# Attention on one Trainium2 core: two heads' scores in one tile of two banks, with one exponential over both

## The chip, the cores and the metric

The kernel runs on one core of a Trainium2 chip. The metric is the device time of one execution in microseconds (us), measured from outside the program; a few executions are made and their median is taken. The core has five engines that run at the same time and wait for each other by semaphores: TensorE (PE in the profile; PEld is its loading of weights), VectorE (DVE), ScalarE (ACT), GpSimd (POOL) and SyncE (SP), which here does nothing but start transfers (DMAs). Matmuls write to PSUM, a memory of eight banks; a bank holds 512 fp32 columns of 128 rows.

## The reference

One transformer block in fp32 on 2048 tokens of width 640: layer norm, attention with 32 heads of width 20, a residual sum, layer norm again, a SwiGLU network of width 1728 and a second residual sum. The change touches the attention alone:

```
scores = jnp.einsum("bhqd,bhkd->bhqk", q, k) * (Dh ** -0.5)
p = _softmax(scores, axis=-1)
o = jnp.einsum("bhqk,bhkd->bhqd", p, v)
h = x + o.transpose(0, 2, 1, 3).reshape(B, S, D) @ wo
h2 = h + (silu(ln(h) @ w_gate) * (ln(h) @ w_up)) @ w_down
```

## The kernel before, in words

The program has three stages: projections of queries, keys and values (which also find some of the maxima of the scores), attention, and the SwiGLU network. Each engine executes its instructions in the order in which the Python code issues them.

**Units and steps.** Attention works through 32 units (line 1040): a unit u is a group of four heads (g = u // 4) with 512 queries (c = u % 4). A unit has 16 steps, one for each tile of 128 keys (`kt`, line 1045), so there are 512 steps. In a step the scores of four heads are computed, transposed, as tiles of 128 keys by 512 queries; their exponentials go to two tiles `probs` of two heads each; and the exponentials of two steps earlier are multiplied with the values into `acc` (`weigh`, lines 972 to 980, kept back by the list `todo`).

**Maxima.** The exponential needs the largest score of each query. It is subtracted inside the score matmul: two extra rows of the queries, filled in by `max_finish`, carry the negative maximum as a sum of two parts, and the keys have rows of ones there. So while unit u is being worked on, the maxima of the next units are found: `max_one` (lines 200 to 212) multiplies 128 queries of one head with 512 keys into a bank `ps_max` and VectorE reduces it. After a unit's last maximum `max_all` (214) reduces the parts and negates them, and two steps later `max_finish` (221 to 236) transposes the result on TensorE into a PSUM tile, splits it in two parts on ScalarE and VectorE (`split`, lines 84 to 86) and writes them into the query rows with four DMAs.

**Halves of the array.** Heads are stacked two to a tile: one in rows 0 to 63 and one in rows 64 to 127 (index b = 0 or 1). A score or maximum matmul thus uses one half of TensorE's rows, and the next matmul on the other half can run beside it.

**The order in a step** is written out by hand in `ORDER` (line 41), one string for even and one for odd steps. `W` is the weighing of an older step; directly behind it come a finished maximum's `max_finish`, pieces of other work (`extra`, `preparing`). `s` and `S` are scores of a head with b = 0 and b = 1: `heads` (line 1049) makes them heads 0 and 2, and 1 and 3. `m` and `M` are maxima with b = 0 and 1. When no maxima are left the order is `sSsSW`. Before: `WsSmmSsM` and `WSsMMsSm`.

**Banks.** The attention stage has four single-bank tiles `ps_one` for scores (line 624; `max_finish` takes one as well), three `ps_max`, and one `acc`. Each score matmul (line 964) goes to a `ps_one` of its own and is read by an exponential of 512 columns (line 970). Tiles rotate: the fifth score waits until the exponential of the first is done.

**Other work that meets these steps.** After a unit's last weighing ScalarE copies `acc` to `o` (line 984); `max_finish` puts a small copy on ScalarE; POOL prepares the weights of the network; in the last units the output projection (lines 663 to 754) runs in the steps, with `ps_max` as its PSUM.

Of the kernel before, what the change touches and what calls it, by code (L numbers as in the profile page):

```python
# [9 lines left out]
F32 = mybir.dt.float32  # L10
# [3 lines left out]
AF = mybir.ActivationFunctionType  # L14
# [3 lines left out]
P = 128  # L18
# [7 lines left out]
CH = 512  # L26
NC = S // CH
TPC = CH // P
NF = (F + P - 1) // P
G = 4  # L30
# [7 lines left out]
LOWEST = -3.4028234e38  # L38
GD = G * DH

ORDER = ("WsSmmSsM", "WSsMMsSm")


@with_exitstack
def tile_block(ctx: ExitStack, tc: tile.TileContext, x, wqkv, wo, wg, wu, wd, out):
    nc = tc.nc
# [24 lines left out]
    psum = ps_ctx.enter_context(tc.tile_pool(name="psum", bufs=1, space=bass.MemoryType.PSUM))  # L71
# [4 lines left out]
    def ps_one():  # L76
        return psum.tile([P, CH], F32, name="ps_one", tag="ps_one", bufs=2)
# [6 lines left out]
    def split(src, hi, lo, lo_engine=nc.vector):  # L84
        nc.scalar.activation(hi, src, AF.Copy)  # L85
        lo_engine.tensor_tensor(out=lo, in0=src, in1=hi.bitcast(F32), op=ALU.subtract)  # L86
# [133 lines left out]

    def max_finish(u):

        m = ps_one()[: G * TPC, :P]
        nc.tensor.transpose(m, ends.pop(u), ident)
        parts = stk.tile([G * TPC, 2, P], F32R, name="m2", tag="m2", bufs=1)
        split(m, parts[:, 0], parts[:, 1], nc.vector)
        for b in range(2):
            for i in range(2):
                row = b * ROW + NPART + i
                first = b * 2 * TPC  # L230
                nc.sync.dma_start(
                    queries[u][row : row + 1].bitcast(F32).rearrange(
                        "r j (t p) -> r (j t) p", t=TPC
                    ),
                    parts[first : first + 2 * TPC, i, :].bitcast(F32),
                )
# [31 lines left out]
    with tc.tile_pool(name="pa", bufs=2) as pa:  # L268
# [138 lines left out]
        def flip(c, k):  # L407
            ps = ps_one()
            for t in range(TPC):
                nc.tensor.transpose(  # L410
                    ps[:, t * P : (t + 1) * P], xs[c * TPC + t][:, k * P : (k + 1) * P], ident
                )
            z_hi, z_lo = (z[:, k, :] for z in zs[c])
            split_sbuf(ps, z_hi, z_lo, next_e()[:, 0, :CH].bitcast(F32))
# [19 lines left out]
        def query_key(c, m):  # L434

            z_hi, z_lo = zs[c]
            ps = ps_wide()[:, 0, :] if slot[0] < 6 else ps_one()
            for n, (a, w) in enumerate(((z_hi, w_hi), (z_lo, w_hi), (z_hi, w_lo))):
                for k in range(ND):
                    nc.tensor.matmul(  # L440
                        ps, w[:, k, m * P : (m + 1) * P], a[:, k, :],
                        start=(n == 0 and k == 0), stop=(n == 2 and k == ND - 1),
                    )
                    if n == 1 and k == 3 and c:
                        visit(3)
            keep(c, m, ps)
# [117 lines left out]
        for c in range(NC):  # L564
# [7 lines left out]
            for j, (kind, *which) in enumerate(work):  # L572
# [27 lines left out]
                if 0 in ends:  # L600
                    finish_at = min(finish_at, slot[0] + 2)
                    if slot[0] == finish_at:
                        max_finish(0)
# [17 lines left out]
    ps_ctx = ExitStack()  # L621
    psum = ps_ctx.enter_context(tc.tile_pool(name="psum_a", bufs=1, space=bass.MemoryType.PSUM))

    def ps_one():
        return psum.tile([P, CH], F32, name="ps_one", tag="ps_one", bufs=4)

    def ps_max():
        return psum.tile([P, CH], F32, name="ps_max", tag="ps_max", bufs=3)
# [327 lines left out]
    v_stk.append(pb.tile([P, NT, VG], F32, name="v_stk1", bufs=1))  # L956
    scale = 1.0 / math.sqrt(DH)

    def scores(u, kt, j, probs):

        p, b = divmod(j, 2)
        rows = slice(b * ROW, b * ROW + NPART + 2)
        ps = ps_one()
        nc.tensor.matmul(  # L964
            ps,
            keys[u // NC][rows, p, kt * P : (kt + 1) * P],
            queries[u][rows, p, :],
            start=True, stop=True,
        )
        nc.scalar.activation(probs[p][:, b, :], ps, AF.Exp, scale=scale)  # L970

    def weigh(u, kt, probs, acc):
        for j in range(G):
# [66 lines left out]
    for u in range(NU):  # L1040
# [4 lines left out]
        for kt in range(NT):  # L1045
            now[0] = u * NT + kt
            ready = [v for v, at in closing.items() if at == now[0]]
            probs = [pp.tile([P, 2, CH], F32, name="probs") for _ in range(2)]
            heads = [[0, 2], [1, 3]]
            order = ORDER[now[0] % 2] if singles[0] or singles[1] else "sSsSW"  # L1050
            for op in order:
                if op in "mM":
                    next_max(int(op == "M"))
                elif op in "sS":
                    scores(u, kt, heads[op == "S"].pop(0), probs)
                else:
                    if len(todo) == 2:
                        weigh_next()
                    for v in ready:
                        max_finish(v)  # L1060
                    if extra:
                        extra.pop(0)()
                    if preparing and u and kt not in (3, 4):
                        preparing.pop(0)()
                    if now[0] == (NU - NC) * NT + 8:
                        unit_ring, last_ring = weight_rings()
                        unit_ring.fill()
                        last_ring.fill()
# [41 lines left out]
    u, o, r = tail.pop()  # L1110
# [561 lines left out]
```

## Time and profile before

| what | value |
|---|---|
| time, median of 3 runs | 2104.36 us (2101.28 to 2106.47; the runs: 2106.47, 2101.28, 2104.36) |
| span of the profiled execution, first to last instruction | 2102.6 us (the profile gives no other time of that execution) |
| instructions of the core | 37159 |
| exponentials (line 970) | 2048, 614 ns each |
| score matmuls (line 964) | 2048, 450 ns each |
| maxima: matmuls (line 204), reductions (line 210) | 1472 each, 425 and 684 ns |
| weighing (line 974) | 4096 matmul records, 604 ns each |
| output copies (line 984) | 32, 628 ns each |
| TensorE clock | full (mean 0.996) |

How to read it: the page of the profile gives the busy time of each engine, the chain of work that ended last, and groups of instructions by line. In a group's row stand the line, the engine, the operation, output and inputs, shapes and count; behind the first bar the busy time in us and the mean of one in ns; behind the second the idle time of the engine just before, with what ended it ("<-"). The mean of one is longer than the distance between two, since neighbours overlap. A row of the timeline has the start in us from the start of the span, the duration, the engine, the line and the operation; equal neighbours are merged (x2), and idle time ahead of it stands in brackets. A row of the windows has for each engine (PE, PEld, DVE, ACT, POOL) the busy time in us and the number of instructions.

### The profile page before, as it was taken

The page shows a single profiled execution, that of the slowest core. Times are in us where ns is not written, and L with a number is a line of the kernel's source. Part 1 is how long each engine was busy: PE and PEld are TensorE (multiplying, and loading weights), DVE is VectorE, ACT ScalarE, POOL GpSimd, SP SyncE. Part 2 cuts the span into 40 slices and gives each one's busy share as a digit, 9 for nine tenths or more (in the row PEclk, how much of TensorE's full clock was granted, in tenths as well). Part 3 has the DMA queues.
Part 4 walks back from the last instruction along what each step waited for, and adds up shares of the span by engine and source line. Part 5 has one row for each costly group of instructions (what it writes and reads, how often), then busy time and mean ns, then how long its engine had stood idle before and what let it go on. Part 6 is the DMA issues. An engine that isn't in the chain of part 4 may idle for free.

```text
span 2102.6 us, 37159 instructions
## 1 busy us (share of the span) xinstructions
PE 2063.2 (98%) x12636; PEld 1204.5 (57%) x12636; DVE 1659.2 (79%) x3631; ACT 1444.6 (69%) x2835; POOL 691.8 (33%) x949
## 2 busy tenths in 40 slices
PE   8899999999999999999999999999999999999998
PEld 6656566443333343333333333335578888888888
DVE  7677867788888888888888988887358666666677
ACT  4556575899999999999999999996743222212221
POOL 2131210234443434353420001001145444753555
PEclk9999999999999999999999999999999999999999
DMA  8575544335263443443631213132137755884542
GB/s 256 165 230 168 175 127 132 85 115 154 88 184 101 148 138 124 148 147 122 187 124 57 52 32 94 34 94 83 35 122 274 257 176 183 300 302 157 196 153 92
DMA packets 197285, 305.38 MB, mean 145 GB/s; under 512 B 47440, under 2 KB 82256, under 8 KB 196072
## 3 DMA queue, kind: packets, MB, share of 16 engines
q1 hardware_dynamic: 186168, 280.18, 42.0%
q10 hardware_dynamic: 10928, 22.82, 3.5%
q8 instruction: 102, 1.67, 0.3%
q14 instruction: 87, 0.71, 0.1%
HBM read 203.82 MB, written 98.30 MB: 144 GB/s over the span
## 4 chain that ended last, share of the span: by engine, by line
PE 88%; DVE 4%; DMA 3%; issue 1%; ACT 1%; POOL 1%; SPq 1%; ACTq 0%; POOLq 0%; DVEq 0%
PE acc L974 24%; PE ps_one L964 16%; PE ps_a L1135 15%; PE ps_max L204 12%; PE ps_b L1229 8%; PE ps_one L516 3%; PE ps_one L440 3%; PE ps_wide L188 3%; DVE over L195 2%; PE ps_max L695 2%; PE ps_b L695 1%; PE ps_wide L440 1%; DMA k_d<-e 1%; DMA halves<-j_d 1%; DVE mx L180 1%
## 5 line engine op out<-in xcount | busy, mean ns | idle before, releaser
L970 ACT ACTIVATE probs<-ps_one 128x512 f32<-128x512 f32 x2048 | 1056.7, 614 | 62.5 <-PE ps_one L964 37.1
L210 DVE TENSOR_REDUCE mx<-ps_max 128x1 f32<-128x512 f32 x1472 | 925.9, 684 | 108.2 <-PE ps_one L964 75.6
L964 PE MATMUL ps_one<-q_stk,k_stk 62*128 62x512 f32 x2048 | 586.1, 450 | 2.5 <-DVE m L86 1.8
L974 PE MATMUL acc<-probs,v_stk 128*32 128x512 f32 x4096 | 545.2, 604 | 0.0
L964 PEld LDWEIGHTS ps_one<-q_stk,k_stk 62*128 62x128 f32 x2048 | 251.3, 184 | 431.5 <-ACT probs L970 397.2
L204 PE MATMUL ps_max<-k_stk,q_stk 60*128 60x512 f32 x1472 | 380.8, 425 | 0.0
L204 PEld LDWEIGHTS ps_max<-k_stk,q_stk 60*128 60x128 f32 x1472 | 271.6, 186 | 25.3 <-DVE mx L210 1.2
L195 DVE CUSTOM_DVE_ANT_0 over<-ps_wide,over 128x256 f32<-128x256 f32 x512 | 185.4, 420 | 86.3 <-ACT over L193 85.9
L1350 DVE TENSOR_TENSOR tmp<-ps_a,tmp 128x512 f32<-128x512 f32 x208 | 141.1, 689 | 119.7 <-PE ps_a L1135 93.9
L193 ACT ACTIVATE over<-ps_wide 128x512 f32<-128x512 f32 x256 | 139.1, 597 | 90.5 <-PE ps_wide L188 44.1
L1229 PE MATMUL ps_b<-halves,yp 128*128 128x320 f32 x1032 | 179.3, 308 | 1.9 <-POOL yp L86 1.2
L974 PEld LDWEIGHTS acc<-probs,v_stk 128*32 128x32 f32 x4096 | 80.6, 108 | 175.4 <-issue 166.8
L1229 PEld LDWEIGHTS ps_b<-halves,yp 128*128 128x128 f32 x1032 | 165.1, 188 | 18.6 <-POOL yp L86 1.5
L1009 POOL TENSOR_TENSOR o<-o,rb 128x512 f32<-128x512 f32 x31 | 39.9, 1287 | 411.5 <-DMA q_stk<-q_d 163.6
L1135 PE MATMUL ps_a<-t,units 128*128 128x512 f32 x624 | 162.6, 396 | 0.0
L1135 PE MATMUL ps_a<-z,units 128*128 128x512 f32 x516 | 133.8, 394 | 0.0
L1135 PEld LDWEIGHTS ps_a<-t,units 128*128 128x128 f32 x624 | 112.6, 188 | 18.6
L86 POOL TENSOR_TENSOR yp<-y,yp 128x256 fp32r<-128x256 f32 x96 | 60.3, 628 | 188.0 <-ACT yp L85 188.0
L1234 DVE TENSOR_TENSOR h<-ps_b,h 128x320 f32<-128x320 f32 x248 | 110.0, 481 | 6.9 <-PE ps_b L1229 5.4
L1135 PEld LDWEIGHTS ps_a<-z,units 128*128 128x128 f32 x516 | 93.1, 187 | 15.9
L85 ACT ACTIVATE yp<-tmp 128x512 fp32r<-128x512 f32 x40 | 25.3, 632 | 103.2 <-POOL tmp L1222 103.2
L1135 PE MATMUL ps_a<-z,lasts 128*128 128x512 f32 x324 | 92.5, 393 | 0.0
(193 smaller groups left out, 2216.4 us busy)
## 6 DMA issues: line engine op xcount, KB each, us to landing
units<-w_d SPq DMA_DIRECT2D x186, 256.0 KB
w_d<-stage SPq DMA_DIRECT2D x106, 256.0 KB
halves<-j_d SPq DMA_DIRECT2D x70, 320.0 KB
j_d<-stage SPq DMA_DIRECT2D x42, 320.0 KB
k_stk<-k_d SPq DMA_DIRECT2D x64, 160.0 KB
q_stk<-q_d SPq DMA_DIRECT2D x64, 160.0 KB
rb<-r_d SPq DMA_DIRECT2D x32, 256.0 KB
raw<-k_d SPq DMA_DIRECT2D x42, 160.0 KB
```

The source lines that it names most:

```text
L193: nc.scalar.activation(over, ps[:, :, CH // 2 :], AF.Relu)
L195: nc.vector.tensor_tensor_reduce(over[:, b], ps[:, b, : CH // 2], over[:, b], 1.0, LOWEST, ALU.add, ALU.max, mx[:, b, pair, t, kc : kc + 1],)
L204: nc.tensor.matmul(ps, queries[u][rows, pair, t * P : (t + 1) * P], keys[u // NC][rows, pair, kc * CH : (kc + 1) * CH], start=True, stop=True,
L210: nc.vector.tensor_reduce(mxs[u][:, b, pair, t, kc : kc + 1], ps, axis=AX.X, op=ALU.max)
L440: nc.tensor.matmul(ps, w[:, k, m * P : (m + 1) * P], a[:, k, :], start=(n == 0 and k == 0), stop=(n == 2 and k == ND - 1),)
L964: nc.tensor.matmul(ps, keys[u // NC][rows, p, kt * P : (kt + 1) * P], queries[u][rows, p, :], start=True, stop=True,)
L970: nc.scalar.activation(probs[p][:, b, :], ps, AF.Exp, scale=scale)
L974: nc.tensor.matmul(acc[32 * j : 32 * j + 32, :], values[u // NC][:, kt, j * VW : j * VW + 32], probs[j // 2][:, j % 2, :], start=(kt == 0) ...
L1135: nc.tensor.matmul(ps.rearrange("p (t n) -> p t n", t=TPC), w[k][:, i], z[k][:, :, j], start=(first and m == 0), stop=(last and m == len(n ...
L1229: nc.tensor.matmul(ps, a, b, start=(n == 0), stop=(n == len(pairs) - 1))
L1234: nc.vector.tensor_tensor(out=h, in0=ps, in1=h, op=ALU.add)
L1350: add = lambda out, ps, x: nc.vector.tensor_tensor(out=out, in0=ps, in1=x, op=ALU.add)
```

## The change

The four single-bank tiles become two tiles of two banks, `ps_two`. The two scores that follow each other in a step, heads 0 and 1 and then heads 2 and 3, share one: each head has a bank. The first of the two takes the tile, the second is followed by one exponential of 1024 columns over both, which writes a whole `probs` tile. `both` is the list in which the function remembers the open tile. The order of a step is changed so that two maxima stand between the score pairs and one behind them. In the attention stage `max_finish` takes a `ps_max` for its transpose; the call for unit 0, which is in the stage of the projections, keeps `ps_one`. Nothing else differs.

```diff
-ORDER = ("WsSmmSsM", "WSsMMsSm")
+ORDER = ("WsSmMsSm", "WSsMmSsM")
...
     def max_finish(u):
 
-        m = ps_one()[: G * TPC, :P]
+        m = (ps_max() if u else ps_one())[: G * TPC, :P]
         nc.tensor.transpose(m, ends.pop(u), ident)
...
-    def ps_one():
-        return psum.tile([P, CH], F32, name="ps_one", tag="ps_one", bufs=4)
+    def ps_two():
+        return psum.tile([P, 2, CH], F32, name="ps_two", tag="ps_two", bufs=2)
 
     def ps_max():
         return psum.tile([P, CH], F32, name="ps_max", tag="ps_max", bufs=3)
...
+    both = []
+
     def scores(u, kt, j, probs):
 
         p, b = divmod(j, 2)
         rows = slice(b * ROW, b * ROW + NPART + 2)
-        ps = ps_one()
+        if not both:
+            both.append(ps_two())
+        else:
+            both.append(None)
+        ps = both[0]
         nc.tensor.matmul(
-            ps,
+            ps[:, b, :],
             keys[u // NC][rows, p, kt * P : (kt + 1) * P],
             queries[u][rows, p, :],
             start=True, stop=True,
         )
-        nc.scalar.activation(probs[p][:, b, :], ps, AF.Exp, scale=scale)
+        if len(both) == 2:
+            nc.scalar.activation(probs[p], ps, AF.Exp, scale=scale)
+            both.clear()
```

## The prediction

> **What bounds the kernel now.** I read the page first (engines, chain of waits, groups), then a window over the attention stage, then single steps in the timeline.
>
> ```profile
> PE 2063.2 (98%) x12636; PEld 1204.5 (57%) x12636; DVE 1659.2 (79%) x3631; ACT 1444.6 (69%) x2835; POOL 691.8 (33%) x949
> ...
> PE 88%; DVE 4%; DMA 3%; issue 1%; ACT 1%; POOL 1%; SPq 1%; ACTq 0%; POOLq 0%; DVEq 0%
> ...
> L970 ACT ACTIVATE probs<-ps_one 128x512 f32<-128x512 f32 x2048 | 1056.7, 614 | 62.5 <-PE ps_one L964 37.1
> L210 DVE TENSOR_REDUCE mx<-ps_max 128x1 f32<-128x512 f32 x1472 | 925.9, 684 | 108.2 <-PE ps_one L964 75.6
> ```
> ```profile
> 391.62:1425.80 1034.18, 1032.40 (x7201) 407.29 (x7200) 919.76 (x1524) 1003.34 (x1977) 295.61 (x460) 1.00 0.37 112
> ```
>
> In the attention stage, PE, ACT and DVE are busy 100%, 97% and 89% (1032.40, 1003.34, 919.76 of 1034.18 us): three candidates, so the shares decide nothing. So long a share of busy time on three engines only says that their work overlaps; which one sets the pace has to be read from a single step. The changed code acts only here; 1472 maxima at three a step are 490 steps. One steady step, PE first, then weight loads, then one exponential that ends before the step's scores, the first that waits for them, and the last reduction of the step before:
>
> ```profile
> 1000.78 1.06 PE L974 MATMUL acc<-probs,v_stk 128*32 128x512 f32 x8
> 1001.77 0.50 PE L964 MATMUL ps_one<-q_stk,k_stk 62*128 62x512 f32 x2
> 1002.11 0.39 PE L204 MATMUL ps_max<-k_stk,q_stk 60*128 60x512 f32 x1
> 1002.11 0.39 PE L964 MATMUL ps_one<-q_stk,k_stk 62*128 62x512 f32 x1
> 1002.34 0.50 PE L204 MATMUL ps_max<-k_stk,q_stk 60*128 60x512 f32 x2
> 1002.58 0.40 PE L964 MATMUL ps_one<-q_stk,k_stk 62*128 62x512 f32 x1
> 1002.91 0.64 PE L974 MATMUL acc<-probs,v_stk 128*32 128x512 f32 x4
> ```
> ```profile
> 1002.12 0.19 PEld L204 LDWEIGHTS ps_max<-k_stk,q_stk 60*128 60x128 f32 x1
> 1002.35 0.18 PEld L964 LDWEIGHTS ps_one<-q_stk,k_stk 62*128 62x128 f32 x1
> 1002.35 0.18 PEld L204 LDWEIGHTS ps_max<-k_stk,q_stk 60*128 60x128 f32 x1
> ```
> ```profile
> 1001.15 0.60 ACT L970 ACTIVATE probs<-ps_one 128x512 f32<-128x512 f32 x1
> ...
> 1002.31 0.60 ACT L970 ACTIVATE probs<-ps_one 128x512 f32<-128x512 f32 x1
> ```
> ```profile
> 1001.62 0.68 DVE L210 TENSOR_REDUCE mx<-ps_max 128x1 f32<-128x512 f32 x1
> ```
>
> A step is 2.13 (1000.78 to 1002.91). Call 1001.77 zero. Scores and maxima on rows 0 and 64 of the array run beside each other, so the seven matmuls take four slots, at 0, 0.34, 0.57 and 0.81, then the weighing at 1.13 (0.32 after slot 4), then 0.99 to the next zero. Slot 2 comes 0.34 after slot 1, later slots 0.23 apart: a weight load issued only when it is wanted delays its matmul by 0.11. So a matmul of slot n may have its load as late as the slot's time less 0.11, here 0.46 for slot 3 and 0.70 for slot 4. The third maximum's load, at 0.58, comes 0.05 after the reduction that frees its bank (1001.62+0.68=1002.30): 0.05 is a release. It is late but harmless.
>
> Is zero itself set by ACT? A step in which ACT is behind, and one in which DVE is:
>
> ```profile
> 425.11 0.63 ACT L984 ACTIVATE o<-acc 128x512 f32<-128x512 f32 x1
> 425.59 3.58 ACT L970 ACTIVATE probs<-ps_one 128x512 f32<-128x512 f32 x7
> ...
> 425.59 0.64 ACT L970 ACTIVATE probs<-ps_one 128x512 f32<-128x512 f32 x1
> 426.06 0.65 ACT L970 ACTIVATE probs<-ps_one 128x512 f32<-128x512 f32 x1
> ```
> ```profile
> 425.91 1.06 PE L974 MATMUL acc<-probs,v_stk 128*32 128x512 f32 x8
> ...
> 426.90 0.18 PEld L964 LDWEIGHTS ps_one<-q_stk,k_stk 62*128 62x128 f32 x2 [0.84 <-ACT probs L970]
> ...
> 427.75 0.18 PEld L964 LDWEIGHTS ps_one<-q_stk,k_stk 62*128 62x128 f32 x1 [0.31 <-ACT probs L970]
> ...
> 428.18 1.06 PE L974 MATMUL acc<-probs,v_stk 128*32 128x512 f32 x8
> ```
> ```profile
> 434.53 1.06 PE L974 MATMUL acc<-probs,v_stk 128*32 128x512 f32 x8
> ...
> 436.37 0.18 PEld L204 LDWEIGHTS ps_max<-k_stk,q_stk 60*128 60x128 f32 x1
> 436.37 0.49 PE L204 MATMUL ps_max<-k_stk,q_stk 60*128 60x512 f32 x1
> 436.79 0.16 PEld L974 LDWEIGHTS acc<-probs,v_stk 128*32 128x32 f32 x8 [0.24 <-issue]
> ```
>
> The last exponential to end before zero ended 0.02 earlier in the steady step (1001.75) and 0.19 earlier in the other (426.71 against 426.90), and weighing to zero was 0.99 both times. So the "0.84 <-ACT" there is a label on time that PE spent weighing, not a wait. A real wait is 427.75: load at 0.85, 0.11 more is 0.96 against 0.81, and that step is 2.27, 0.14 longer. Likewise 436.37 waits for DVE (finishing a unit's maximum, L217, sits ahead of the reductions): step 2.26. I take PE's own slots as the bound, ACT and DVE close behind.
>
> Beside this: the Trainium skill, "Trainium Kernel Development and Optimization", section "Best Practices", says that busy time of pipelined matmuls is no measure of the bound and that busy weight loads are. By that rule PE at 39% (407.29 of 1034.18) is free and ACT binds, which is the last rival below. The fixed 0.99 speaks against it here.
>
> **The change, part by part.** *PE's order.* s and m use one half of the array, S and M the other. The old order puts s m m s on one half and S S M on the other; the new one s m s m and S M S (mirrored in each other step). The fuller half has four matmuls either way, so four slots and 2.13: **0**. A moved maximum brings its matmul and its reduction along; the reductions still run in their old sequence of three a step, on DVE alone. A unit's last maximum issues the finishing reduction, and two steps later the transpose, its split on ACT and DVE and four row loads on SP; those stay in the step in which they were. SP and POOL keep their order, and ACT issues no DMA in this stage. If the cover were incomplete and a fifth slot appeared, it would cost 0.23 a step; nothing in the two halves calls for one.
>
> *The exponential.* Its price at 1024 columns is in no row. Nearest are
>
> ```profile
> L193 ACT ACTIVATE over<-ps_wide 128x512 f32<-128x512 f32 x256 | 139.1, 597 | 90.5 <-PE ps_wide L188 44.1 <-issue 25.0 <-DVE mx L195 7.4
> ...
> L180 DVE TENSOR_REDUCE mx<-ps_wide 128x2 f32<-128x1024 f32 x32 | 38.9, 1220 | 3.2 <-PE ps_wide L176 3.2
> ...
> L85 ACT ACTIVATE z_hi<-ps_wide 128x640 fp32r<-128x640 f32 x4 | 2.6, 705 | 4.4 <-PE ps_wide L420 4.4
> ```
>
> Back to back, an exponential of 512 costs 0.49: seven end at 429.17, the first at 426.23, 2.94/6. From 512 to 640 columns, across two banks, is 108 ns, so 512 more cost 0.43 (L180's second bank added only 536 ns to L210's 684). I take 0.92 back to back, 1.03 alone. Bounds: 0.86 (columns alone, 2x0.43) and 0.98 (nothing saved, 2x0.49). I take the middle because the 640-column row shows columns and a fixed part separately. ACT's load in a step falls from 4x0.49=1.96 to 2x0.92=1.84, but this lies beside PE's 2.13: **0** directly.
>
> By the Trainium skill, "ScalarE: Activation LUTs", section "What ACT_TABLE_LOAD costs" (186 ns plus 0.833 ns a column, 93 ns overlapped), 1024 columns would cost an estimated 0.95. The trace's 0.49 for 512 is under that page's 0.52. With 0.95 the chain below would be 2.13, just no slack left.
>
> *The new wait.* There are two tiles of two banks. Call the first score pair of a step A and the second B. A's tile was last read by the A exponential of the step before, B's by the B exponential, and only the first score of a pair carries the wait. A's exponential starts 0.54 after zero (1002.31, as the first one does now) and ends at 0.54+0.60+0.43=1.57, long before the next A. B's follows at once and ends 0.92 later, at 2.49; its banks are released at 2.54, which is 0.41 in the next step. B is in slot 3, and its load may come as late as 0.46: **0**, hidden behind the maxima of slot 2, with 0.05 to spare. Without that cover every 0.01 costs 490x0.01=5 us. Behind it on PE stand B's second score, the third maximum and the weighing. As a loop over two steps: release 0.05, load 0.11, slot 3 to 4 0.24, to the weighing 0.32, to zero 0.99, to the end of B's exponential 2.49: 4.20, or 2.10 a step under 2.13. This is the thin place of the forecast: 0.03 more per long exponential uses it up. The third maximum now has until 0.70 for its bank, which comes at 0.58.
>
> *What is late now and then.* (a) Finishing reductions, 32 in all:
>
> ```profile
> L217 DVE TENSOR_REDUCE neg<-mx 128x16 f32<-128x64 f32 x32 | 7.0, 220 | 1.1
> ```
>
> The 0.13 that one costs at 436.37 falls within the third maximum's new margin (0.12). At most 32x0.13=4; where it falls before a free moment of DVE nothing was lost, so I take half: **-2**. (b) After an output copy (425.11): ACT then ends B's exponential at 2.49-2.13+0.49+1.84=2.69, +0.05=2.74, against 2.13+0.46=2.59: 0.15 late, as now 0.14: **0**. (c) A finished maximum's transpose takes one of three ps_max banks instead of one of four ps_one; now the third maximum, not a score, waits for its split. Where the output copy is just ahead:
>
> ```profile
> 527.21 1.07 PE L974 MATMUL acc<-probs,v_stk 128*32 128x512 f32 x8
> ...
> 529.63 0.18 PEld L964 LDWEIGHTS ps_one<-q_stk,k_stk 62*128 62x128 f32 x1 [0.69 <-DVE m L86]
> ...
> 530.07 1.07 PE L974 MATMUL acc<-probs,v_stk 128*32 128x512 f32 x8
> ```
>
> This step takes 2.86. The same split stands behind ACT's queue, which the new order ends at 2.49-2.13=0.36; the old one ends it at 0.54+0.60+3x0.49-2.13=0.48. That is 0.12 sooner, at each of 7 changes of head group: **-1**. Elsewhere the transpose's bank is freed by the same split as now, in time for the same slot 4: **0**. (d) The 21 steps without maxima: now 4x0.49=1.96; the new loop is 4.20-0.24=3.96 per two, 1.98: under **0.5**.
>
> Sum: 0-2-1+0.5, about **-3**. Against the profiled span of 2102.6 that is 2099.6; the runs' median, 2104.36, lies 1.8 above that span, and so I forecast **2101**.
>
> **The rivals.** *B, the late third maximum costs.* Some steps are shorter:
>
> ```profile
> 501.32 1.06 PE L974 MATMUL acc<-probs,v_stk 128*32 128x512 f32 x8
> ...
> 503.43 0.64 PE L974 MATMUL acc<-probs,v_stk 128*32 128x512 f32 x4
> ```
>
> This is 2.11. If the late load at 0.58 is what makes 2.13 of it, the new order gives up to 490x0.02=10 back: 2101-10=**2091**. Against it: by the 0.11 rule that load is 0.12 early. *C, slower: the two-bank ring.* If the long exponential saves nothing (0.98), the loop is (4.20+0.12)/2=2.16, 0.03 over the step: 490x0.03=15, **2116**. It decides from about 0.95 on; place: pair B's load, behind expB. For it: slack is thin, a score now has two places where it had four. Against: L193 and the 640-column row. *D, ACT was the bound.* Then 490x(1.96-1.84)=59 come off, the change does what it says: about **2045**; the constant 0.99 is against it. *E*: B's load waits longer than 0.05 or pairs hold up the maxima, over **2116**.
>
> **How the numbers follow.** 2101 is the likeliest: 0.48; B 0.19; C 0.21; D 0.05; E 0.07. The range goes from B's end less a little to C's, 2090 to 2116; D, E and edges left out are under 0.2. About 0.3%, 6 us, is what a measurement of this kernel can tell from no change. Faster by more: D, most of B and a little of the forecast, 0.27; slower: E, two thirds of C, a little of the forecast, 0.23; within: 0.50.
>
> **What would show it.** Right: steps still near 2.13, weighing to first score 0.99, B's weight load near 0.41 and its matmul at 0.57, ACT's long exponentials about 0.92 apart where saturated and ACT idle some 0.3 a step; steps with finishing reductions at 2.13. Wrong: B's load past 0.46 with "ACT probs" as its releaser (C or E), steps at 2.11 (B), steps well under 2.10 (D).

## The result, and the profile after

The changed kernel takes 2107.82 us (median of 14 runs, 2106.21 to 2113.68), the kernel before in the same measurement 2103.99 (14 runs, 2101.28 to 2106.47): a ratio of 1.0018, 95% interval [1.0011, 1.0025]. The time lies in the forecast range and within 0.3% of the old one, but on the other side: 4 us more where 3 fewer were forecast. The two profiled spans differ by as much (2106.6 against 2102.6). In the changed kernel the lines have moved: scores are L970, the exponential L977, the weighing L982, the output copy L992.

The page of the kernel after: busy times, the chain of work, the exponential and the reduction of a maximum.

```profile
PE 2062.9 (98%) x12636; PEld 1170.1 (56%) x12636; DVE 1661.5 (79%) x3631; ACT 1383.5 (66%) x1811; POOL 691.9 (33%) x949
...
PE 85%; DMA 4%; DVE 4%; ACT 2%; issue 2%; POOL 1%; SPq 1%; ACTq 0%; DVEq 0%; POOLq 0%
...
L977 ACT ACTIVATE probs<-ps_two 128x1024 f32<-128x1024 f32 x1024 | 992.2, 1024 | 125.5 <-PE ps_two L970 122.9
L210 DVE TENSOR_REDUCE mx<-ps_max 128x1 f32<-128x512 f32 x1472 | 926.5, 684 | 110.8 <-PE ps_max L204 106.5
```

ACT has 1024 exponentials fewer and 61 us less to do, DVE and PE as much as before, and the time is longer. So ACT's work was not the bound.

To compare kernels to a few tenths of a microsecond I use one window from here on: from the third weighing of the attention stage to the 479th, 476 steps. The first numbers of a row are its length and PE's busy time, the 1.00 behind POOL's is PE's clock. Before, and after:

```profile
395.87:1425.81 1029.94, 1028.16 (x7172) 405.58 (x7171) 916.20 (x1518) 999.31 (x1970) 291.41 (x459) 1.00 0.37 111
```
```profile
396.27:1429.70 1033.43, 1032.54 (x7171) 374.46 (x7170) 916.32 (x1518) 942.64 (x1018) 291.06 (x460) 1.00 0.37 111
```

These 476 steps, the main steps, are 3.5 us longer: nearly the whole difference. From the 479th weighing to the last but one are 32 steps more, in which the output projection runs; they went from 109.15 to 108.40 (0.75 less, all of it in those of them that have no maxima). The first weighing comes 0.4 later, and 0.8 is lost behind the attention: 3.5 - 0.75 + 0.4 + 0.8 = 3.95, the difference of the spans.

A steady step of the kernel after, PE, then the weight load of the second pair (B), then ACT:

```profile
404.76 1.06 PE L982 MATMUL acc<-probs,v_stk 128*32 128x512 f32 x8
405.76 0.50 PE L970 MATMUL ps_two<-q_stk,k_stk 62*128 62x512 f32 x2
406.09 0.40 PE L204 MATMUL ps_max<-k_stk,q_stk 60*128 60x512 f32 x2
406.33 0.40 PE L970 MATMUL ps_two<-q_stk,k_stk 62*128 62x512 f32 x2
406.58 0.39 PE L204 MATMUL ps_max<-k_stk,q_stk 60*128 60x512 f32 x1
406.89 0.64 PE L982 MATMUL acc<-probs,v_stk 128*32 128x512 f32 x4
```
```profile
406.22 0.19 PEld L970 LDWEIGHTS ps_two<-q_stk,k_stk 62*128 62x128 f32 x2 [0.17 <-ACT probs L977]
```
```profile
406.36 1.94 ACT L977 ACTIVATE probs<-ps_two 128x1024 f32<-128x1024 f32 x2 [0.19 <-PE ps_two L970]
```

The step is 2.13 (404.76 to 406.89) and weighing to zero 1.00 (405.76), as before. The slots stand at 0, 0.33, 0.57 and 0.82: four, as forecast. Two exponentials take 1.94, so the second ends 0.92 behind the first: as forecast. One number is not: the first exponential starts at 406.36, **0.60** after zero instead of 0.54. Hence B's load comes at 0.46 (406.22), waiting for ACT: exactly at its limit of 0.46, where the forecast had it at 0.41. Over all steps in which ACT was idle ahead of it, the first exponential starts a median of 0.604 after its pair's first weight load, at 0.542 in the experiments below that remove the cause.

The cause is in the trace's raw records, which the views leave out (semaphore instructions do not count as busy). ACT in this step, start and end in us, and what the record waits for:

```
406.296 406.313  EVENT_SEMAPHORE  L977   waits on PE (ACT's sequencer)
406.358 407.381  ACTIVATE         L977   waits on ACT
406.778 406.795  EVENT_SEMAPHORE  L977   waits on PE (ACT's sequencer)
407.279 408.297  ACTIVATE         L977   waits on ACT
```

Each long exponential waits for two semaphores: PE's, for its scores, and ACT's own, for the exponential six back that wrote the same `probs` tile. In the kernel before each of the 2048 exponentials waits for PE's alone. The second wait is long fulfilled, but with two waits the program has an instruction of its own ahead of the exponential, and that one takes the wait for PE. It ends at 406.313, and the exponential starts 0.045 later. In the 476 steps the kernel after has 1109 such instructions on ACT, 952 of them ahead of its 952 long exponentials; the kernel before has 169, none of them ahead of an exponential. (The Trainium skill, "Perfetto Trace Analysis", section "Identifying Dependency Chains", says that an instruction that waits on several engines may get such instructions ahead of it; this trace agrees. Here it costs 0.06.)

Sorting the 476 steps by what happens in them shows where the rest went. Each cell is how much the steps of a kind take over 2.125 each, in us, so that a column's sum plus 476 x 2.125 = 1011.5 is the window. A step in which two of these things happen stands in one row only. The four experiments are told below.

| kind of step (number) | before | after | order alone | tiny copy | order, late end | both, fewer copies |
|---|---|---|---|---|---|---|
| finishing reduction L217 (29-30) | 1.87 | 2.96 | 3.09 | 3.01 | -0.05 | -0.03 |
| transpose of a finished maximum (30) | 10.89 | 10.60 | 10.95 | 10.18 | 10.85 | 10.26 |
| output copy in the step (22) | 0.07 | 0.48 | 0.06 | -0.01 | 0.16 | -0.02 |
| behind an output copy (29) | 3.28 | 4.53 | 3.59 | 5.56 | 3.56 | 3.65 |
| split of a network weight on ACT (8) | 1.82 | 1.02 | 1.83 | 1.49 | 1.82 | 1.62 |
| lone long steps of 2.40 | 0 | 1.12 (4) | 0 | 0 | 0 | 0 |
| all others (353-358) | 0.51 | 1.22 | 0.19 | -0.65 | -0.01 | -0.30 |

### The profile page after: what moved, and what is told of

The parts are those of the page before. It is cut to its first block, busy times and chain, and to the rows that moved or that the text cites. A ratio compares the mean times of both kernels' runs of the same rounds, so it can differ in the third digit from the quotient of the medians.

```text
span 2106.6 us, 37126 instructions
## 1 busy us (share of the span) xinstructions
PE 2062.9 (98%) x12636; PEld 1170.1 (56%) x12636; DVE 1661.5 (79%) x3631; ACT 1383.5 (66%) x1811; POOL 691.9 (33%) x949
## 4 chain that ended last, share of the span: by engine, by line
PE 85%; DMA 4%; DVE 4%; ACT 2%; issue 2%; POOL 1%; SPq 1%; ACTq 0%; DVEq 0%; POOLq 0%
PE acc L982 23%; PE ps_two L970 15%; PE ps_a L1143 14%; PE ps_max L204 11%; PE ps_b L1237 8%; PE ps_one L516 3%; PE ps_one L440 3%; PE ps_wide L188 3%; DVE over L195 2%; PE ps_max L695 2%; ACT probs L977 1%; PE ps_b L695 1%; PE ps_wide L440 1%; DMA halves<-j_d 1%; DVE mx L180 1%
## 5 line engine op out<-in xcount | busy, mean ns | idle before, releaser
L977 ACT ACTIVATE probs<-ps_two 128x1024 f32<-128x1024 f32 x1024 | 992.2, 1024 | 125.5 <-PE ps_two L970 122.9
L982 PE MATMUL acc<-probs,v_stk 128*32 128x512 f32 x4096 | 545.2, 604 | 0.0
L970 PE MATMUL ps_two<-q_stk,k_stk 62*128 62x512 f32 x2048 | 465.8, 451 | 3.8 <-ACT probs L977 2.9
L970 PEld LDWEIGHTS ps_two<-q_stk,k_stk 62*128 62x128 f32 x2048 | 191.7, 183 | 474.2 <-ACT probs L977 459.4
L204 PE MATMUL ps_max<-k_stk,q_stk 60*128 60x512 f32 x1472 | 394.2, 397 | 0.7
L204 PEld LDWEIGHTS ps_max<-k_stk,q_stk 60*128 60x128 f32 x1472 | 190.8, 186 | 17.4 <-DVE m L86 8.0
L982 PEld LDWEIGHTS acc<-probs,v_stk 128*32 128x32 f32 x4096 | 80.5, 108 | 177.3 <-issue 169.0
```

The costliest lines, as they stand in the source:

```text
L204: nc.tensor.matmul(ps, queries[u][rows, pair, t * P : (t + 1) * P], keys[u // NC][rows, pair, kc * CH : (kc + 1) * CH], start=True, stop=True,
L970: nc.tensor.matmul(ps[:, b, :], keys[u // NC][rows, p, kt * P : (kt + 1) * P], queries[u][rows, p, :], start=True, stop=True,)
L977: nc.scalar.activation(probs[p], ps, AF.Exp, scale=scale)
L982: nc.tensor.matmul(acc[32 * j : 32 * j + 32, :], values[u // NC][:, kt, j * VW : j * VW + 32], probs[j // 2][:, j % 2, :], start=(kt == 0) ...
```

## The experiments

**The theories.** T1: the second wait starts each pair's first exponential 0.06 late, which uses up the reserve of the ring of two tiles. T2: the new place of the maxima costs. T3: two tiles are too short by themselves, whatever the wait. The first four kernels were run together (before there: 2105.3, 29 runs), then the next four (2104.82, 33 runs), then the last (2104.53, 15 runs); each experiment has 11 or 12 runs, the fourth 4. One profiled execution stands behind each window.

**1. The order alone.** The kernel before with the new order; exponentials of 512 columns, four single banks.

```diff
-ORDER = ("WsSmmSsM", "WSsMMsSm")
+ORDER = ("WsSmMsSm", "WSsMmSsM")
```

> The kernel before with only the new order of a step: four single banks, exponentials of 512, the transpose in ps_one. Theory 1 (the pair's exponential starts 0.07 us late, because it now carries a second wait, and the ring of two tiles has no reserve for that): the order is worth nothing, 0 to +1 us against before, steps at 2.13. Theory 2 (the new place of the maxima costs: finishing reductions now always hold up the third maximum): +3 us. Theory 3 (the ring of two tiles is too short whatever the wait): as before, 0.

Measured: 2106.7 us, ratio 1.0009 [1.0001, 1.0018]. Its window:

```profile
395.08:1426.29 1031.21, 1029.33 (x7171) 423.21 (x7170) 916.60 (x1518) 1000.65 (x1970) 291.73 (x459) 1.00 0.37 111
```

1.27 over before, 1.22 of it in the steps with a finishing reduction (1.87 to 3.09): steps of over 2.20 among the 30 with one in the 478 went from 15 to 23. Such a step in the kernel after, on DVE, then two weight loads (the first score's, at zero, and the third maximum's), then the weighings around it:

```profile
410.79 1.29 DVE L210 TENSOR_REDUCE mx<-ps_max 128x1 f32<-128x512 f32 x2 [0.24 <-PE ps_max L204]
412.11 0.22 DVE L217 TENSOR_REDUCE neg<-mx 128x16 f32<-128x64 f32 x1
412.25 2.56 DVE L210 TENSOR_REDUCE mx<-ps_max 128x1 f32<-128x512 f32 x4
```
```profile
412.15 0.18 PEld L970 LDWEIGHTS ps_two<-q_stk,k_stk 62*128 62x128 f32 x2 [0.84 <-ACT probs L977]
...
412.98 0.18 PEld L204 LDWEIGHTS ps_max<-k_stk,q_stk 60*128 60x128 f32 x1 [0.19 <-DVE mx L210]
```
```profile
411.15 1.06 PE L982 MATMUL acc<-probs,v_stk 128*32 128x512 f32 x8
...
413.41 1.06 PE L982 MATMUL acc<-probs,v_stk 128*32 128x512 f32 x8
```

Two reductions take 1.29 and one 0.68, so the next starts 0.61 after its neighbour: the third was due at 410.79 + 2 x 0.61 = 412.01 and started at 412.25. It is 0.24 late, because the finishing reduction begins only when the one ahead of it, whose result it reads, has ended (410.79 + 1.29 = 412.08), where two of the others overlap by 0.08. The third maximum's load stands at 0.83 (412.98 against 412.15), 0.13 past its limit of 0.70, and the step is 2.26. So the margin of 0.12 takes up half of 0.24, no more. And the order moves work to that place: in eight odd steps the unit's last maximum, `m`, was the step's third before (`MMsSm`), with DVE's idle time behind it; now it is the second (`MmSsM`), with a reduction behind it. T2 is true for this part: 1.2 us.

**2. The old order in the changed kernel.** The same edit, the other way round.

> The changed kernel with the old order of a step. Theory 1 and theory 3: as the changed kernel, +3 to +5 us against before, first exponential 0.60 after the weight load of its pair. Theory 2: as before, 0 to +1 us.

Measured: 2108.33, ratio 1.0016 [1.0007, 1.0025]; the window is

```profile
396.86:1429.42 1032.56, 1032.51 (x7171) 428.50 (x7171) 916.60 (x1518) 942.37 (x1018) 291.65 (x460) 1.00 0.37 111
```

0.87 under after, by the steps with a finishing reduction (2.96 to 1.97); steps behind an output copy keep their 4.54, and the first exponential starts 0.606 after its pair's weight load. So the order isn't the main part: 2.2 to 2.6 us of the 3.5 belong to the exponentials.

**3. The second wait taken away.** A tiny copy of one column of the last step's `probs` runs ahead of each step's first exponential. ACT's own semaphore is then waited for by the copy, and the exponentials wait for PE alone. The copy's result isn't used.

```diff
         if len(both) == 2:
+            if p == 0 and todo:
+                nc.scalar.activation(
+                    pp.tile([P, 1], F32, name="seen", bufs=2), todo[-1][2][0][:, 0, :1], AF.Copy
+                )
             nc.scalar.activation(probs[p], ps, AF.Exp, scale=scale)
```

> The changed kernel with one ScalarE instruction more in a step: ahead of the first exponential, one column of the previous step's probs is copied to a scratch tile. It brings ScalarE's knowledge of its own work up to date, so that the exponentials themselves carry one wait instead of two. Theory 1: the first exponential starts 0.54 after its pair's weight load instead of 0.60, B's weight load comes at 0.41 instead of 0.46, and the time falls by about 3 us against the changed kernel, to before or 1 us under it. Theory 2: no change against the changed kernel. Theory 3: 0 to 1 us less than the changed kernel at best.

Measured: 2105.37, ratio 1.0005 [0.9996, 1.0013]. Its first two steps, and the window behind them:

```profile
392.98:399.73 6.75, 6.75 (x32) 2.24 (x31) 3.05 (x6) 3.43 (x6) 5.29 (x2) 0.60 0.39 123
399.73:1430.80 1031.07, 1030.42 (x7172) 393.75 (x7171) 916.59 (x1518) 983.81 (x1494) 290.10 (x459) 1.00 0.37 111
```

The clock granted to PE was 0.60 over the first two steps of this execution (6.75 instead of 4.25); that is why all windows begin behind them. Over the 476, 2.36 is recovered. A steady step, PE, B's load, ACT:

```profile
1002.32 0.50 PE L970 MATMUL ps_two<-q_stk,k_stk 62*128 62x512 f32 x2
```
```profile
1002.73 0.19 PEld L970 LDWEIGHTS ps_two<-q_stk,k_stk 62*128 62x128 f32 x2
```
```profile
1002.57 0.20 ACT L978 ACTIVATE seen<-probs 128x1 f32<-128x1 f32 x1
1002.86 1.94 ACT L981 ACTIVATE probs<-ps_two 128x1024 f32<-128x1024 f32 x2
```

The exponential starts 0.54 after zero (1002.86 - 1002.32), B's load stands at 0.41 and waits for nobody: the forecast's own numbers. The lone long steps of 2.40 are gone too. T1 holds, with one blemish: in the steps behind an output copy ACT has no idle moment, the copy's 0.20 is added to its queue, and they cost 5.56 instead of 4.53.

**4. The ring made longer.** Each pair's exponential as two of 512 columns, still with two tiles.

```diff
-            nc.scalar.activation(probs[p], ps, AF.Exp, scale=scale)
+            for i in (b ^ 1, b):
+                nc.scalar.activation(probs[p][:, i, :], ps[:, i, :], AF.Exp, scale=scale)
```

> The changed kernel with two exponentials of 512 columns behind each pair, in place of one of 1024: tiles, order and transpose as in the changed kernel; these exponentials carry no second wait. The loop of the prediction, 4.20 us for two steps with 0.92 for a long exponential, becomes 4.32 with 0.98 for two short ones. If the loop is right (theories 1 and 3), steps are 2.16 and the time is +12 to +16 us against before. If PE's slots alone set the step (theory 2), it is within 1 us of the changed kernel.

Measured: 2134.37, ratio 1.0145 [1.0131, 1.0158]: twice the effect expected. The window, some weighings of it, and B's loads in the first two of their steps:

```profile
395.73:1454.16 1058.43, 1055.24 (x7172) 371.33 (x7171) 916.77 (x1518) 998.42 (x1970) 291.33 (x460) 1.00 0.36 108
```
```profile
999.80 1.06 PE L983 MATMUL acc<-probs,v_stk 128*32 128x512 f32 x8
...
1002.06 1.06 PE L983 MATMUL acc<-probs,v_stk 128*32 128x512 f32 x8
...
1004.18 1.06 PE L983 MATMUL acc<-probs,v_stk 128*32 128x512 f32 x8
...
1006.45 1.06 PE L983 MATMUL acc<-probs,v_stk 128*32 128x512 f32 x8
```
```profile
1001.39 0.19 PEld L970 LDWEIGHTS ps_two<-q_stk,k_stk 62*128 62x128 f32 x2 [0.30 <-ACT probs L978]
...
1003.51 0.19 PEld L970 LDWEIGHTS ps_two<-q_stk,k_stk 62*128 62x128 f32 x2 [0.16 <-ACT probs L978]
```

Steps of 2.26 and 2.12 take turns, mean 2.19: B's load is past its limit in one (0.60 after the zero at 1000.79), on it in the next (0.46 after 1003.05). The forecast's loop gives just this if the second wait is counted: B ends at 0.60 + 0.60 + 3x0.49 = 2.67, so 0.05 + 0.11 + 0.24 + 0.32 + 0.99 + 2.67 = 4.38, or 2.19 a step. My expectation had these exponentials without a second wait; the records have it at the first exponential of nearly every pair, with its 0.06. So the loop over two steps is the right model, and for the kernel after it gives 0.60 + 1.03 + 0.92 = 2.55 and 4.26, or 2.13 a step: level with PE's own slots.

**5. The finishing reduction moved to the end of the step** (in the changed kernel), so that it falls into DVE's idle time behind the third reduction.

```diff
+    over = []
...
             if left[a[0]] == 0:
-                max_all(a[0])
+                over.append(a[0])
...
+            while over:
+                max_all(over.pop())
             todo.append((u, kt, probs))
```

> The changed kernel, with the finishing reduction of a unit's maximum issued behind the last reduction of its step instead of between the second and the third. In the changed kernel the 30 steps with such a reduction cost 2.95 us together over their neighbours (23 of them at about 2.26 instead of 2.13). Theory 1 (the second wait of the pair's exponential, and the ring of two tiles, make the slower time; the finishing reduction is a small thing beside them): the 478 main steps go from 1037.7 to about 1034.8, the steps after an output copy stay at 2.32, the whole is 2105. Theory 2 (the new place of the maxima is what costs): the stage falls back to that of before or lower, 1032 or less, because the third maximum is no longer late anywhere. Theory 3 (the ring alone is too short): as theory 1.

Measured: 2104.93, ratio 1.0004 [0.9995, 1.0013]. The window, again behind two slow steps at a clock of 0.59, and the reduction in its new place, with the weighings:

```profile
400.12:1430.95 1030.83, 1029.88 (x7171) 372.52 (x7170) 914.44 (x1518) 940.61 (x1018) 289.54 (x459) 1.00 0.37 111
```
```profile
414.66 1.89 DVE L210 TENSOR_REDUCE mx<-ps_max 128x1 f32<-128x512 f32 x3 [0.24 <-PE ps_max L204]
416.46 0.21 DVE L217 TENSOR_REDUCE neg<-mx 128x16 f32<-128x64 f32 x1
416.79 1.89 DVE L210 TENSOR_REDUCE mx<-ps_max 128x1 f32<-128x512 f32 x3
```
```profile
415.01 1.06 PE L982 MATMUL acc<-probs,v_stk 128*32 128x512 f32 x8
...
417.14 1.06 PE L982 MATMUL acc<-probs,v_stk 128*32 128x512 f32 x8
```

2.60 less; the step is 2.13. The finishing reduction starts at 416.46, 0.09 before the reduction ahead of it ends (414.66 + 1.89 = 416.55): that one's result is not among those it reads. So it is in 23 of the 30 steps. In the other 7 the unit's last maximum is the third of its step, and it starts 0.03 after the end, as in all 30 of the kernel after. Steps behind an output copy still cost 4.66: the two causes are separate, and T2 doesn't reach the second.

**6 and 8. The same move in the kernel before, with the old order and with the new.**

> The kernel before, with the same deferral of the finishing reduction. There the steps with it cost 2.39 us together. All theories: the 478 main steps go from 1034.2 to about 1032.0, the whole from 2104 to 2102. It is the base for the two others: if the gain is the same as in the changed kernel, the finishing reduction explains none of the difference but what the new order added (about 0.6 to 1.2 us).

> The kernel before with the new order of scores and maxima and the deferred finishing reduction, exponentials of 512 columns. Theory 1: the order in itself costs nothing once the finishing reduction is out of the way: the 478 main steps fall from the 1035.5 of the new order alone to about 1032, level with the old order with the deferral. Theory 2: the order costs more than the finishing reduction, the steps stay at 1034 or more.

Measured: 2101.25, ratio 0.9985 [0.9976, 0.9994], and 2101.01, ratio 0.9984 [0.9975, 0.9993]. Windows, old order and new:

```profile
396.15:1423.83 1027.68, 1025.89 (x7171) 402.83 (x7170) 914.99 (x1518) 997.26 (x1970) 291.16 (x459) 1.00 0.37 111
```
```profile
396.32:1424.14 1027.82, 1025.99 (x7171) 419.92 (x7170) 914.40 (x1518) 997.27 (x1970) 291.10 (x459) 1.00 0.37 111
```

With the finishing reduction out of the way, the orders differ by 0.14: the order costs nothing else, and T2 falls beyond that part. Both are faster than the kernel before, their intervals lying below 1, and so than the kernel after.

**7. Both mendings in the changed kernel** (3 and 5).

> The changed kernel with both mendings: a tiny copy of one column ahead of each step's first exponential (so that the long exponentials wait for the matmul alone) and the deferred finishing reduction. Theory 1: the two gains add, the 478 main steps at about 1033.6 - 2.7 = 1030.9, the whole near 2102 to 2103, that is under the kernel before by 1 to 3 us and level with the kernel before with the deferral alone (1032.0). Theory 3: the ring leaves the stage above that of before with the deferral, 1033 or more. Theory 2: as with the deferral alone in the changed kernel, about 1032, for the copy would be worth nothing.

Measured: 2102.88, ratio 0.9991 [0.9983, 1.0]; the window is

```profile
393.77:1422.00 1028.23, 1027.61 (x7171) 393.27 (x7170) 914.41 (x1518) 982.19 (x1494) 291.14 (x460) 1.00 0.37 111
```

5.20 under after, where the gains one by one were 2.36 and 2.60. That is 0.4 over the same order with short exponentials (1027.82). The steps behind an output copy alone are 1.84 over it, so they leave open whether two tiles are too short there, or the tiny copy is in the way.

**9. As 7, without the tiny copy in the two steps from an output copy on.**

```diff
-            if p == 0 and todo:
+            if p == 0 and todo and kt not in (1, 2):
```

> As the kernel with both mendings, but without the tiny copy in the two steps from an output copy on, where ACT has no idle moment to hide it in. Theory 1 (the long exponential costs nothing of its own once it starts on time): the steps after an output copy, 2.36 with the tiny copy in them and 2.28 with exponentials of 512, fall to 2.27 to 2.32; the 478 main steps go from 1032.5 to about 1031.2, under the 1032.1 of the same order with short exponentials, and the whole to about 2101. Theory 3 (two tiles are too short by themselves): those steps stay at 2.36 and the stage at 1032.5.

Measured: 2101.02, ratio 0.9982 [0.9973, 0.9991]; the window is

```profile
399.28:1425.95 1026.67, 1026.03 (x7172) 392.94 (x7171) 914.78 (x1518) 980.22 (x1436) 289.67 (x460) 1.00 0.37 111
```

Steps behind an output copy cost 3.65, as with exponentials of 512 (3.56): the tiny copy had been in the way. T3 falls: the ring by itself costs nothing in this kernel. All in all the long exponential, started on time, is worth 1.15 of 1027.82 here and 0.6 in the 32 steps behind (109.00 to 108.41): less than these runs can tell (2101.02 against 2101.01).

## Why the prediction was wrong

**What bounds the kernel: right.** PE's four slots set the step. ACT lost 57 us of work in the window (999.31 to 942.64), and the window grew. That settles the rival in which ACT was the bound. The Trainium skill ("Trainium Kernel Development and Optimization", section "Best Practices") says to judge how near TensorE is to its limit by the share of peak arithmetic and by busy weight loads, not by busy matmuls; by it, the prediction said, PE would be free and ACT would bind. This trace does not bear that out: weight loads were busy 36% (374.46 of 1033.43), and PE's slots set the step all the same.

**The long exponential: right.** 0.915 back to back (median), 1.02 alone; 0.92 and 1.03 were taken. The 0.95 estimated from the Trainium skill ("ScalarE: Activation LUTs", section "What ACT_TABLE_LOAD costs") was too high for this case.

**The step that failed is "A's exponential starts 0.54 after zero (1002.31, as the first one does now)".** It starts at 0.60. I carried the start of the old exponential over to the new one, though the new one stands in another relation to its scores: with one exponential for two matmuls the program no longer takes ACT's earlier write of that buffer as covered by the wait for PE, adds a second wait and an instruction for it. Why the wait on the pair's second matmul doesn't cover it, I read from the program as that matmul having no wait of its own (in the records of the step above its weight load waits for nothing, where in the steady step of the kernel before each score's load waits for ACT); no run tested that part. The forecast had called 0.05 its thin place, priced 0.03 a step and exponential, and looked for the risk in the exponential's length alone. The price in the window, after against the order alone: 0.4 in steps with an output copy, 1.0 in the steady ones, 0.9 behind output copies, and 1.1 in the lone long steps. Other kinds gave back 1.3, so that 2.2 is left.

**(b) After an output copy, "0.15 late as now 0.14": 0. Wrong by the same 0.06.** Median 2.27 before, 2.32 after. The copy queues behind an exponential that ends 0.06 later. With the second wait gone the steps cost 3.65 against 3.56: then the step of the forecast holds.

**(a) Finishing reductions, -2: wrong in sign, +1.1.** This term is as large a part of the miss as the late start. The sum took 0.13 for what one costs, which is what is left of 0.24 after a margin, and set it against the third maximum's margin of 0.12 as if it were the whole; that margin was there before, and the 0.13 was what stood out over it. And "half, where it falls before a free moment of DVE" was right for the old order (15 of 30) but not for the new one (23 of 30 with the order alone, 21 in the kernel after).

**(c) -1: mis-sized.** The 30 steps with a transpose gained 0.3 in all; without the second wait, 0.7 (10.89 to 10.18), 0.5 of it at the seven changes of head group that the forecast had meant.

**(d) Under 0.5: the wrong sign.** The last steps without maxima gained 0.75; in some of them ACT sets the pace (1.96 with four short exponentials, 1.84 with two long ones). So did the 8 steps with a weight's split on ACT, which the forecast had not looked at: 0.8. These gains of a lighter ACT hid part of the loss.

**The rivals.** B (the late third maximum makes 2.13 of 2.11) falls: the steps without anything special average 2.126 before and 2.125 with the new order and the late end. C had the place right (B's load, behind the second exponential), the cause wrong (the exponential did save what was forecast), and the price too high: the loop ended level with PE's 2.13 and not 0.03 above. Experiment 4 is C carried out, at its price.

By kinds, after against before: finishing reductions 1.1, behind copies 1.25 (0.3 of it with the order alone), transposes -0.3, all others 0.7, copies 0.4, lone long steps 1.1, splits -0.8; that is 3.5 in the main steps, where the forecast had -3 (-2 and -1). Of the miss of 6.5, (a) is 3.1, (c) 0.7, and the late start together with the steps behind copies 3.5, less the 0.8 of the splits. That the time fell into the range is owed to the width of the range, not to the sum.

## What to carry to other kernels

When one instruction takes the place of two, write down anew what it waits for and in which order its conditions come true; its start can't be taken over from the old one, and a reserve of a few hundredths of a microsecond in a ring must be priced against that too. A short reduction issued directly behind the one whose result it reads costs its engine more than the lengthening of a step shows (0.24 here, where the step grew by 0.13): ask where in the step it is issued, for an order that moves the instruction it hangs on moves it as well. Here moving that reduction by a few lines of Python gave 2.3 to 3.4 us of the main steps, more than the 1.15 that the long exponential was worth there once it started on time.

## What the runs showed of the hardware

- In the kernel after, a long exponential's wait for PE, the later of its two, stands on a separate instruction ahead of it: 0.017 for that, 0.045 to the start, 0.06 later in all (0.604 against 0.542).
- Five times in the main steps of the kernel after, the gap from that instruction to the exponential was 0.33 instead of 0.045. The first, with 0.47 instead of 0.19 idle ahead of the exponential:

```profile
443.77 3.78 ACT L977 ACTIVATE probs<-ps_two 128x1024 f32<-128x1024 f32 x4 [0.47 <-PE ps_max L204]
```

  The next step then takes 2.40; four of the five are the lone long steps of the table. Experiments 2 and 5 have four such steps as well (1.10 and 1.09 us), the three with the tiny copy none. The places are not random: the extra instruction stands behind 958, 1726, 1854, 2238 and 2878 recorded instructions of ACT, the same in experiments 2 and 5, and these numbers differ by multiples of 128. The one such gap of experiment 4, behind 3262, fits as well. What ACT's sequencer does there stays open.
- The finishing reduction (64 columns) starts 0.034 after the end of the reduction of 512 columns ahead of it where it reads what that one wrote, in all 30 steps of the kernel after, and 0.08 before that end where it doesn't, in 23 of 30 in experiment 5. Two reductions of 512 columns, of which neither reads the other's result, overlap by 0.08.
- The start of the attention stage ran at a granted clock of 0.60, 0.59 and 0.75 for two steps in three of the profiled executions, with no difference in the work; up to 2.6 us of a span come and go that way.
